# A Mamba-2 scan and a low-rank mixer on one core: U, V and the first weights loaded in another order

## The chip, the core and the metric

The kernel runs on one NeuronCore of a Trainium2 chip. The metric is the device time of one execution in microseconds (us); a kernel's time is the median of its runs. Five engines work beside each other, each through its own instruction stream in order: PE multiplies matrices, DVE and ACT work on elements, POOL does the same more slowly, and SP issues the DMAs. An instruction at the head of an engine's stream that waits holds up everything behind it on that engine.

## The reference

Four sequences (`batch` 4) with 8 heads, 768 positions, head dimension 32 and state size 16 go through a chunked state-space scan; its output is the input of a mixer:

```python
cum = np.cumsum(log_a[chunk]);  L = exp(cum_i - cum_j) * causal
y   = ((C @ B^T) * L) @ x  +  (C @ state) * exp(cum)
state = exp(sum) * state + sum_j B_j x_j * exp(cum_end - cum_j)
# y: (4, 768, 256) after the heads are joined; U (768, 32), V (32, 768)
h = y^T @ U @ V
u = y + h^T
out = u + max(u @ w_ch1, 0) @ w_ch2        # w_ch1 (256, 1024), w_ch2 (1024, 256)
```

The weights U, V, w_ch1 and w_ch2 come as float64. The kernel loads them as pairs of 32-bit words and turns them into float32 by integer and float operations on DVE and ACT.

## The kernel before, in words

**Pairs.** The scan takes two blocks of 128 positions at a time. There are 12 such pairs, three for each sequence, numbered k = 0 to 11, so "the third pair" is k = 2 and "the fourth" k = 3. The first three (sequence 0) go through a form of the scan with larger products (`LIGHT`).

**A plan of words.** One string, `PLAN`, lists all steps in the order in which they are issued; `follow` goes through it, and there is no other scheduler. Each word is a letter and indices. The words that the change and the prediction speak of:

- loads on SP's queue: `b3.0`, `b3.1`, `b3.2` (B and C of k = 3, lines 205 and 210), `x3.0`, `x3.1` (x of k = 3, line 219), `W0`, `W1` (the two halves of the first quarter of w_ch1), `Z` (V), `z` (U), `w3` and on (the other quarters, 512 KB each);
- scan: `Q` and `P` scale B and C by the decays (line 490), `V` and `T` transpose them on PE and copy them out by ACT (lines 506, 510, 516), `g` forms the grams C B^T (lines 537 and 547), `m` and `M` mask them on DVE (lines 569 and 579; for k < 3 the last quarter of a mask goes over ACT and POOL, lines 563 to 567), `s` and `u` update the state, `n`, `i`, `j` build y, `y` copies it out, `O` and `t` turn it into token order;
- weights: `c0` to `c9` convert words to float32, one of four steps at each mention (lines 438 to 453). `c0` and `c2` are the two halves of the first quarter of w_ch1, `c1` is U and V together;
- mixer: `p0`, `q0` project y by U, `v` spreads V, `a0.0` adds h to y (DVE, "yT" at line 772), and `U0.0.1` and the like are the first products with w_ch1 (line 797, tiles "w1f").

**DMAs.** All loads are issued by SP, one after the other. Each DMA uses one of eight completion semaphores in turn, and waits for the DMA that used it before, so that the ninth transfer cannot be issued before the first has landed. U and V share a tile of words and are converted together, so that `c1` needs both. Before the change:

```python
def load_v():
    own["UV"] = words_of(UV)
    weights[1] = UV, own["UV"]
    for q in range(4):
        begin(out=own["UV"][ts(q, Q), 2 * NC * RK:], in_=V2[:, ts(q, 2 * NC * RK)])
```

Loads whose word is B, X, w or L wait in addition for the last DVE instruction that stands ahead of them in the plan; the words b, x, W, z and Z do not.

Of the kernel before, what the change touches and what calls it, by code (L numbers as in the profile page):

```python
# [38 lines left out]
SETTLED = range(4, 12)  # L39
PLAN = (  # L40
# [46 lines left out]
def kernel(  # L87
# [28 lines left out]
    P = 128  # L116
    NB, NH, S, D = x.shape
    N = B.shape[-1]
    NC = S // P
    NPR = NC // 2  # L120
    DM = NH * D
    RK = moe_U.shape[1]
# [7 lines left out]
    Q = 32  # L130
# [27 lines left out]
    class Kept:  # L158
# [6 lines left out]
        def __getattr__(self, name):  # L165
# [16 lines left out]
        out=a_sb,  # L182
        in_=a.rearrange("(g b) h (c s) -> g (b h c) s", g=2, s=P).rearrange(
            "g r s -> r g s"))
# [4 lines left out]
    def hold(load, until):  # L189

        tc.add_manual_dep(load.ins, until.ins.name, mybir.DependencyInfo(
            mybir.DependencyClass.Sync, mybir.DependencyReason.DATA))

    def begin(**kwargs):
        op = nc.sync.dma_start(**kwargs)  # L195
        if until:
            hold(op, until.pop())
# [26 lines left out]
    UV = const.tile([P, 2, NC * RK], FP32)  # L224
# [8 lines left out]
    w2 = [const.tile([P, NM, DM], FP32R, name=f"w2{i}") for i in range(2)]  # L233
    weights = {}
# [7 lines left out]
    def words_of(dst):  # L242
        p, i, j = dst.shape
        t = raw.tile([P, 2 * WCOLS], INT32, tag="words", name="words", bufs=NWORDS)
        return t[:p, :2 * i * j]
# [11 lines left out]
    U2, V2, w12, w22 = (w.bitcast(INT32) for w in (moe_U, moe_V, moe_w_ch1, moe_w_ch2))  # L257
# [2 lines left out]
    w13 = w12.rearrange("(c p) m -> p c m", p=P)  # L260
    own = {}

    def load_v():
        own["UV"] = words_of(UV)
        weights[1] = UV, own["UV"]
        for q in range(4):
            begin(out=own["UV"][ts(q, Q), 2 * NC * RK:], in_=V2[:, ts(q, 2 * NC * RK)])

    def load_u():
        begin(out=own["UV"][:, :2 * NC * RK].rearrange("p (c r) -> p c r", c=NC),  # L270
                          in_=U2.rearrange("(c p) r -> p c r", p=P))

    def load_w(n):
        if n < 2:
# [13 lines left out]
    def load(k):  # L288
        if k < NB * NPR:
            load_bc(k)  # L290
            load_x(k)

    loads = dict(B=load_bc, X=load_x, w=load_w, b=lambda k, p: load_bc(k, (p,)),
                 x=lambda k, c: load_x(k, (c,)), W=load_w, Z=lambda n: load_v(),
                 z=lambda n: load_u())
    for word in LOADS.split():
        loads[word[0]](*(int(v) for v in word[1:].split(".")))
# [36 lines left out]
    for half in range(2):  # L334
        both = sides[:, half].rearrange("p (g s r) -> p s g r", g=2, s=2)
        for s in range(2):
            nc.gpsimd.tensor_scalar(
                out=both[:, s], in0=same[:, None, :].to_broadcast([P, 2, Q]),
# [10 lines left out]
    for g in range(2):  # L349
# [3 lines left out]
        out=la.rearrange("p b c h -> p b h c"),  # L353
# [577 lines left out]
    def ytokens_kept(k):  # L931
# [9 lines left out]
                 v=spread)  # L941
# [51 lines left out]
```

## Time and profile before

| | |
|---|---|
| median of 3 runs | 218.69 us (217.45 to 219.2) |
| the profiled execution's own time | 216.94 us |
| its span, first to last instruction | 215.1 us |
| mean granted PE clock | 1.0 |
| busy share of the span: PE, DVE, ACT, POOL | 96%, 75%, 56%, 7% |
| DMA | 14.57 MB, 69519 packets, of which 63792 under 512 B |

The span is a little shorter than the execution's time, by what lies before the first and after the last instruction (1.84 us here). A row of the timeline gives start and duration in us, engine, line, operation, tiles with shapes, the count of merged instructions, and in brackets how long the engine had idled before it and what ended that. A row of a window gives the busy time of each engine in it, the granted clock, the mean busy share of the 16 DMA engines and the rate. "L169" is the helper through which every DVE instruction of the kernel is issued.

### The profile page before, as it was taken

What the parts mean: (1) busy time and instruction counts of PE and PEld (TensorE: products, weight loads), DVE (VectorE), ACT (ScalarE), POOL (GpSimd) and SP (SyncE); (2) the same over time, 40 slices, a digit from 0 to 9 for tenths busy, and PEclk for the clock granted to TensorE, in tenths of its full rate; (3) what the DMA queues carried; (4) which work ended last, traced back from release to release, by engine and by line L of the source; (5) the groups of instructions that cost most, each with busy time, mean ns of one, the idle gap of its engine ahead of it and who ended that gap; (6) DMA issues with size and microseconds to landing.
All of it is one profiled execution on the core that took longest, in us unless ns stands there. A gap on an engine that the chain in (4) does not pass through costs nothing.

```text
span 215.1 us, 6853 instructions
## 1 busy us (share of the span) xinstructions
PE 207.0 (96%) x2912; PEld 180.8 (84%) x2912; DVE 161.3 (75%) x334; ACT 119.9 (56%) x273; POOL 14.5 (7%) x46
## 2 busy tenths in 40 slices
PE   7998699999999999999999999999999999999993
PEld 4666465666676989999899999998999999999993
DVE  4679499999999999968977594497347756636942
ACT  3566567896847695655275527433646357357120
POOL 7463210000000000000000000000000000000000
PEclk9999999999999999999999999999999999999999
DMA  5987899998850035002061010100001000100012
GB/s 87 142 184 106 120 202 316 155 265 110 109 80 3 2 66 111 0 3 76 3 81 21 24 49 3 49 27 6 6 0 49 0 27 0 49 29 0 0 50 100
DMA packets 69519, 14.57 MB, mean 68 GB/s; under 512 B 63792, under 2 KB 67696, under 8 KB 69488
## 3 DMA queue, kind: packets, MB, share of 16 engines
q1 hardware_dynamic: 69488, 14.13, 33.6%
q8 instruction: 23, 0.38, 0.8%
q14 instruction: 8, 0.07, 0.1%
HBM read 10.98 MB, written 3.15 MB: 66 GB/s over the span
## 4 chain that ended last, share of the span: by engine, by line
PE 84%; SPq 5%; DMA 4%; DVE 2%; issue 2%; ACT 1%; DVEq 0%
PE x L797 31%; PE z L797 24%; PE y L797 12%; SPq L195 5%; PE y L704 3%; PE y L672 3%; DMA words<-in_moe_w_ch_dram 3%; PE x L547 2%; PE w L728 2%; PE w L506 2%; DMA bc<-in_C_dram 2%; PE w L598 1%; PE w L751 1%; PE z L547 1%; DVE M L169 1%
## 5 line engine op out<-in xcount | busy, mean ns | idle before, releaser
L169 DVE SCALAR_TENSOR_TENSOR words<-words 128x768 fp32r<-128x768 f32 (+6 forms) x48 | 38.0, 818 | 0.7 <-PE y L797 0.5
L797 PE MATMUL z<-u,w 128*128 128x384 f32 x144 | 32.0, 341 | 0.0
L797 PE MATMUL x<-u,w 128*128 128x384 f32 x144 | 31.7, 338 | 0.0
L797 PEld LDWEIGHTS z<-u,w 128*128 128x128 f32 x144 | 24.3, 188 | 0.3 <-issue 0.2
L797 PEld LDWEIGHTS x<-u,w 128*128 128x128 f32 x144 | 24.3, 188 | 0.2
L802 ACT ACTIVATE x<-x 128x384 f32<-128x384 f32 (+1 forms) x32 | 14.3, 448 | 18.1 <-PE x L797 18.1
L802 ACT ACTIVATE z<-z 128x384 f32<-128x384 f32 (+1 forms) x28 | 12.8, 461 | 16.6 <-PE z L797 16.1
L169 DVE SCALAR_TENSOR_TENSOR words<-x,words 128x384 fp32r<-128x384 f32 x24 | 13.1, 553 | 8.7 <-ACT words L831 8.6
L169 DVE SCALAR_TENSOR_TENSOR words<-z,words 128x384 fp32r<-128x384 f32 x24 | 12.9, 552 | 8.9 <-ACT words L831 8.8
L797 PE MATMUL y<-w,words 128*128 128x256 f32 x144 | 19.3, 281 | 0.0
L797 PEld LDWEIGHTS y<-w,words 128*128 128x128 f32 x144 | 18.4, 189 | 0.1
L797 PE MATMUL x<-w,words 128*128 128x256 f32 x128 | 18.3, 281 | 0.0
L797 PE MATMUL x<-w2c,words 128*128 128x256 f32 x96 | 17.6, 317 | 0.0
L797 PEld LDWEIGHTS x<-w,words 128*128 128x128 f32 x128 | 17.0, 188 | 0.2
L797 PEld LDWEIGHTS x<-w2c,words 128*128 128x128 f32 x96 | 14.9, 189 | 1.1
L831 ACT ACTIVATE words<-x 128x384 fp32r<-128x384 f32 x24 | 11.7, 491 | 6.0 <-PE x L797 5.9
L831 ACT ACTIVATE words<-z 128x384 fp32r<-128x384 f32 x24 | 11.6, 492 | 3.0 <-PE z L797 3.0
L169 DVE SCALAR_TENSOR_TENSOR S<-S,kept,w 128x64 f32<-128x64 f32 x40 | 11.1, 278 | 1.6
L797 PE MATMUL z<-yT,w1f 128*128 128x384 f32 x32 | 11.7, 495 | 0.1
L797 PE MATMUL x<-yT,w1f 128*128 128x384 f32 x32 | 11.1, 489 | 0.0
L672 PEld LDWEIGHTS y<-T,Sm 32*64 32x64 f32 x352 | 8.1, 131 | 2.7 <-issue 2.1
L797 PE MATMUL y<-w2c,words 128*128 128x256 f32 x72 | 10.3, 282 | 0.0
(170 smaller groups left out, 398.4 us busy)
## 6 DMA issues: line engine op xcount, KB each, us to landing
words<-in_moe_w_ch_dram SPq DMA_DIRECT2D x7, 512.0 KB, 6.8
x<-in_x_dram SPq DMA_DIRECT2D x24, 128.0 KB, 3.6
out_dram<-ytok SPq DMA_DIRECT2D x24, 128.0 KB, 1.7
bc<-in_B_dram SPq DMA_DIRECT2D x24, 64.0 KB, 3.0
bc<-in_C_dram SPq DMA_DIRECT2D x12, 128.0 KB, 3.1
words<-in_moe_w_ch_dram SPq DMA_DIRECT2D x2, 256.0 KB, 5.5
words<-in_moe_V_dram SPq DMA_DIRECT2D x4, 48.0 KB, 4.8
words<-in_moe_U_dram SPq DMA_DIRECT2D x1, 192.0 KB, 5.0
```

What stands on the lines that cost most here:

```text
L169: self.last = call(*args, **kwargs)
L195: op = nc.sync.dma_start(**kwargs)
L506: nc.tensor.transpose(out=tp[:, i, v], in_=s["BC"][:, i, c + v].rearrange("p h n -> p (h n)"), identity=ident)
L547: nc.tensor.matmul(out=g[r][cols, c], lhsT=s["T"][rows, 0, c, cols], rhs=s["Cm"][rows, :, :, ts(2 * c + p, Q)].rearrange("r v t i -> r v i ...
L598: nc.tensor.matmul(out=s["A"][p][ts(r, Q), v], lhsT=s["BC"][half, 0, v, 2 * r:2 * r + 2].rearrange("p h n -> p (h n)"), rhs=x_sb[k][half, ...
L672: product = nc.tensor.matmul(out=y[at][ts(r % 2, H), c, ts(p, H)] if light else y[p][ts(r % 2, H), r // 2, c], lhsT=own[ts(r, Q)], rhs=s[" ...
L704: product = nc.tensor.matmul(out=y[p][ts(i, Q), n, c], lhsT=x_sb[k][half, c, h], rhs=s["M"][half, h // 2, c, h % 2], start=fresh(k, p, [i] ...
L728: nc.tensor.transpose(out=t[:, c, g], in_=yT[b][:, g, ts(2 * q + c, P)], identity=ident)
L751: nc.tensor.matmul(out=p[ts(i % 4, Q), h], lhsT=U_sb[:, c], rhs=ytok[b][:, c, h], start=i < 4, stop=True, skip_group_check=True)
L797: nc.tensor.matmul(out=t, lhsT=lhsT, rhs=rhs, start=start, stop=True, skip_group_check=True)
L802: nc.scalar.activation(t, t, AF.Copy, scale=1.0 + EPS)
L831: nc.scalar.activation(gs[j, m // 2][0][:, m % 2], t, AF.Relu, scale=NEAR)
```

## The change

The third pair's x (both blocks) is loaded ahead of the two halves of the first quarter of w_ch1. U follows directly, then V, and only then the fourth pair's B, C and x. V comes in one transfer of 192 KB whose source is walked as 4 x 32 rows of 1.5 KB, not in four of 48 KB. Of the 650 words of the plan the 21st to the 197th stand in another order; the words themselves are the same, and from `u6.0` on, shortly ahead of `U0.1.0`, the plan is unchanged.

```diff
     own = {}
 
+    def words_uv():
+        if "UV" not in own:
+            own["UV"] = words_of(UV)
+            weights[1] = UV, own["UV"]
+        return own["UV"]
+
     def load_v():
-        own["UV"] = words_of(UV)
-        weights[1] = UV, own["UV"]
-        for q in range(4):
-            begin(out=own["UV"][ts(q, Q), 2 * NC * RK:], in_=V2[:, ts(q, 2 * NC * RK)])
+        v = words_uv()[:, 2 * NC * RK:]
+        begin(out=v, in_=V2.rearrange("r (q c) -> q r c", q=4))
 
     def load_u():
-        begin(out=own["UV"][:, :2 * NC * RK].rearrange("p (c r) -> p c r", c=NC),
-                          in_=U2.rearrange("(c p) r -> p c r", p=P))
+        begin(out=words_uv()[:, :2 * NC * RK].rearrange("p (c r) -> p c r", c=NC),
+              in_=U2.rearrange("(c p) r -> p c r", p=P))
...
 PLAN = (
...
-    'u0.1 W1 W0 Z0 Q2.2 F2.3 x2.0 F3.3 V1.0.2 b3.2 x2.1 b3.0 Q2.1 b3.1 F3.0 z0 x3.0 x3.1 Q2.0 '
+    'u0.1 x2.0 x2.1 W1 Q2.2 F2.3 W0 F3.3 V1.0.2 z0 Z0 b3.2 Q2.1 b3.0 F3.0 b3.1 x3.0 V1.1.2 Q2.0 '
```

On SP's queue, from the load of the second pair's last x block (`x1.0`) on, the rows were these ("waits" names the semaphore that the row waits for, DMAHW0 to DMAHW7 being those of the DMAs):

```order
L195 DMA x<-in_x_dram 128x8x32 [waits DMAHW5_49]
L195 DMA words<-in_moe_w_ch_dram 128x2x256 [waits DMAHW6_49]
L195 DMA words<-in_moe_w_ch_dram 128x2x256 [waits DMAHW7_49]
L195 DMA words<-in_moe_V_dram 32x384 [waits DMAHW0_49]
L195 DMA words<-in_moe_V_dram 32x384 [waits DMAHW1_49]
L195 DMA words<-in_moe_V_dram 32x384 [waits DMAHW2_49]
L195 DMA words<-in_moe_V_dram 32x384 [waits DMAHW3_49]
L195 DMA x<-in_x_dram 128x8x32 [waits DMAHW4_49]
L195 DMA bc<-in_B_dram 128x8x16 [waits DMAHW5_49]
L195 DMA x<-in_x_dram 128x8x32 [waits DMAHW6_49]
L195 DMA bc<-in_B_dram 128x8x16 [waits DMAHW7_49]
L195 DMA bc<-in_C_dram 128x8x32 [waits DMAHW0_49]
```

Behind the last of them came U and the fourth pair's x, twice. Now the same place reads:

```order
L195 DMA x<-in_x_dram 128x8x32 [waits DMAHW5_49]
L195 DMA x<-in_x_dram 128x8x32 [waits DMAHW6_49]
L195 DMA x<-in_x_dram 128x8x32 [waits DMAHW7_49]
L195 DMA words<-in_moe_w_ch_dram 128x2x256 [waits DMAHW0_49]
L195 DMA words<-in_moe_w_ch_dram 128x2x256 [waits DMAHW1_49]
L195 DMA words<-in_moe_U_dram 128x6x64 [waits DMAHW2_49]
L195 DMA words<-in_moe_V_dram 128x1x384 [waits DMAHW3_49]
L195 DMA bc<-in_B_dram 128x8x16 [waits DMAHW4_49]
L195 DMA bc<-in_B_dram 128x8x16 [waits DMAHW5_49]
L195 DMA bc<-in_C_dram 128x8x32 [waits DMAHW6_49]
L195 DMA x<-in_x_dram 128x8x32 [waits DMAHW7_49]
L195 DMA x<-in_x_dram 128x8x32 [waits DMAHW0_49]
```

U has moved ahead of the fourth pair's B and C, V takes one place of the eight and not four, and the weights have two x blocks in front of them.

On DVE, between the first mask and the conversion of U and V, stood before (masks are the rows with "lower", state updates those of S; 128x256 are `c0` and `c2`, 128x384 is `c1`):

```order
L169 TENSOR_TENSOR words<-z,lower 128x512
L169 TENSOR_TENSOR words<-x,lower 128x512 x2
L169 TENSOR_SCALAR words<-words 128x256 x2
L169 SCALAR_TENSOR_TENSOR S<-S,kept,w 128x64 x2
L169 TENSOR_SCALAR words<-words 128x256 x2
L169 SCALAR_TENSOR_TENSOR S<-S,kept,w 128x64 x2
L169 TENSOR_TENSOR words<-z,lower 128x512
L169 TENSOR_TENSOR words<-x,lower 128x512 x2
L169 SCALAR_TENSOR_TENSOR S<-S,kept,w 128x64 x3
L169 SCALAR_TENSOR_TENSOR words<-words 128x256 x2
L169 TENSOR_SCALAR words<-words 128x384 x2
L169 SCALAR_TENSOR_TENSOR w1f<-words 128x2x128
```

(the first two rows twice, for two pairs). Now:

```order
L169 TENSOR_TENSOR words<-x,lower 128x512 x4
L169 TENSOR_TENSOR words<-z,lower 128x512 x2
L169 SCALAR_TENSOR_TENSOR S<-S,kept,w 128x64 x4
L169 TENSOR_SCALAR words<-words 128x256 x2
L169 TENSOR_TENSOR words<-z,lower 128x512
L169 TENSOR_TENSOR words<-x,lower 128x512 x2
L169 SCALAR_TENSOR_TENSOR S<-S,kept,w 128x64 x2
L169 TENSOR_SCALAR words<-words 128x256 x2
L169 SCALAR_TENSOR_TENSOR S<-S,kept,w 128x64
L169 TENSOR_SCALAR words<-words 128x384 x2
L169 SCALAR_TENSOR_TENSOR words<-words 128x256 x2
L169 SCALAR_TENSOR_TENSOR w1f<-words 128x2x128
```

The first conversion step (`c0`, now the half `W0`) stands behind six masks and four state updates, the second half behind three more masks. From the first mask to the first "yT" addition DVE has the same instructions in both orders.

20 rows, old and new, of the table PLAN are left out of this document.

## The prediction

> **What bounds the kernel now.** I read the busy shares first, then the stages by windows, then what each engine waits for in the one stage that is not full.
>
> ```profile
> PE 207.0 (96%) x2912; PEld 180.8 (84%) x2912; DVE 161.3 (75%) x334; ACT 119.9 (56%) x273; POOL 14.5 (7%) x46
> 12.03:21.81 9.78, 9.02 (x287) 6.33 (x275) 9.15 (x22) 6.59 (x18) 4.32 (x9) 1.00 0.76 151
> 21.81:24.41 2.60, 1.70 (x40) 1.35 (x40) 0.00 (x1) 0.20 (x2) 1.10 (x1) 1.00 0.69 107
> 24.41:32.02 7.61, 6.29 (x176) 4.17 (x176) 7.07 (x20) 5.71 (x16) 0.72 (x2) 1.00 0.97 174
> 12.03:32.02 19.99, 17.00 (x497) 11.86 (x482) 16.22 (x42) 12.50 (x34) 6.14 (x12) 1.00 0.83 154
> 32.64:60.00 27.36, 27.36 (x460) 17.88 (x461) 26.61 (x64) 22.55 (x49) 0.25 (x2) 1.00 0.95 189
> 60.00:200.00 140.00, 140.00 (x1754) 132.53 (x1752) 103.55 (x192) 77.15 (x172) 0.59 (x6) 1.00 0.13 28
> ```
>
> The columns of a window are its length, then busy time of PE, PE's weight loads, DVE, ACT and POOL, the granted clock, the DMA share and GB/s. From 32.64 to 200 us PE is busy without a gap at a clock of 1.00, so whatever lets that stage begin earlier ends the kernel earlier by as much, as long as nothing later runs dry. Before it there is room: in the 19.99 us from DVE's first mask to its first yT addition DVE works 16.22 and idles 3.77, and 2.60 of that is one piece, in which ACT works for only 0.20.
>
> ```profile
> 19.18 0.58 SPq L195 DMA_DIRECT2D words<-in_moe_U_dram  x1
> 24.30 0.55 ACT L442 ACTIVATE words<-words 128x384 f32<-128x384 uint32 x1 [2.40 <-issue]
> 24.41 0.63 DVE L169 TENSOR_SCALAR words<-words 128x384 int32<-128x384 int32 x2 [2.60 <-DMA x<-in_x_dram]
> 25.84 0.60 ACT L510 COPY T<-w 128x512 f32<-128x512 f32 x1
> 27.23 0.35 PE L547 MATMUL x<-Cm,T 32*64 32x128 f32 x2 [0.68 <-ACT Cm L516]
> 28.12 0.76 DVE L169 TENSOR_TENSOR M<-z,causal 128x256 int32<-128x256 int32 x2 [0.30 <-PE z L547]
> 32.02 0.56 DVE L169 TENSOR_TENSOR yT<-x,yT 128x384 f32<-128x384 f32 x1
> 32.64 1.56 PE L797 MATMUL z<-yT,w1f 128*128 128x384 f32 x4
> words<-in_moe_U_dram SPq DMA_DIRECT2D x1, 192.0 KB, 5.0
> ```
>
> Both engines wait at `c1`, the conversion of U and V (128x384). The profile names the x transfer, but that is of other data. U was issued at 19.18 and takes 5.0, so it lands at about 24.2, and ACT and DVE go on at 24.30 and 24.41. Behind `c1` in ACT's stream stands the copy of the fourth pair's transpose (25.84); its gram on PE waits for that (27.23), and the gram's masks on DVE (28.12) are on the way to yT (32.02), after which the first mixer product starts (32.64).
>
> **Why U is late.**
>
> ```profile
> 9.82 0.66 SPq L195 DMA_DIRECT2D x<-in_x_dram  x1
> 10.52 1.09 SPq L195 DMA_DIRECT2D words<-in_moe_w_ch_dram  x2
> 11.66 2.69 SPq L195 DMA_DIRECT2D words<-in_moe_V_dram  x4
> 16.05 0.98 SPq L195 DMA_DIRECT2D x<-in_x_dram  x1
> 18.55 0.58 SPq L195 DMA_DIRECT2D bc<-in_C_dram  x1
> 19.81 1.74 SPq L195 DMA_DIRECT2D x<-in_x_dram  x2
> 21.66 2.28 SPq L195 DMA_DIRECT2D bc<-in_B_dram  x1
> 10.52 5.51 DMA words<-in_moe_w_ch_dram
> 16.05 0.45 ACT L442 ACTIVATE words<-words 128x256 f32<-128x256 uint32 x1 [0.79 <-DMA words<-in_moe_w_ch_dram]
> 16.75 0.44 ACT L442 ACTIVATE words<-words 128x256 f32<-128x256 uint32 x1 [0.25 <-DMA words<-in_moe_w_ch_dram]
> ```
>
> Four V issues cost SP 2.69 us and four of the eight places. The x block at 16.05 stands eight places behind the first weight half, and leaves when that has landed (10.52 + 5.51 = 16.03). U is issued only after it and three more transfers.
>
> **The change part by part.** *U and V earlier.* In the new queue eight places before U lies the third pair's C, long landed, so U needs no landing to be issued: two x blocks and two weight halves after 10.52 at about 0.55 to 0.66 each put it at 13 us, 6 earlier. With the 5.0 it takes now it lands at 18, with another 2 for traffic at 20; V follows it. DVE comes to `c1` at about 21.0 (worked out below, under the weights). The 2.60 wait goes: **-2.60**.
>
> *One transfer for four.* SP saves three issues, 3 x 0.67 = 2.0 us; U's 0.58 now stands ahead of the fourth pair's C. So C is issued near 18.55 - 2.0 + 0.6 = 17.1 and lands 3.54 later, at 20.7 and not at 22.1.
>
> ```profile
> 18.55 3.54 DMA bc<-in_C_dram
> 22.22 1.10 POOL L490 TENSOR_TENSOR BC<-bc,F 128x512 f32<-128x512 f32 x1 [0.70 <-DMA bc<-in_C_dram]
> 25.26 0.35 PE L598 MATMUL w<-x,BC 64*32 64x64 f32 x16 [0.16 <-DMA x<-in_x_dram]
> 5.00:10.00 5.00, 4.57 (x60) 3.38 (x59) 3.31 (x11) 2.43 (x8) 2.32 (x8) 1.00 1.08 150
> 12.00:16.00 4.00, 4.00 (x134) 2.77 (x126) 3.68 (x6) 2.76 (x8) 2.22 (x5) 1.00 0.74 198
> 34.00:36.00 2.00, 2.00 (x8) 1.17 (x7) 1.90 (x4) 1.66 (x4) 0.00 (x0) 1.00 1.04 392
> ```
>
> POOL's scaling (22.22) and the fourth pair's state products, which wait for x (25.26), move up by 1 to 2 us with it. With ACT no longer held at `c1` the gram is there when DVE comes to its masks, so the 0.30 at 28.12 goes too: **-0.30**. If it does not, 0.
>
> *Weights behind the third pair's x.* This is the price. Two x blocks, 262 KB, now pass ahead of `W1` and `W0`. At the 150 GB/s of the stretch in which the DMA engines were full (5 to 10 us, share 1.08) that is 1.75 us; but from 12 to 16 us the engines were only 0.74 busy, and about 1.0 us of it falls into that gap. I take 0.75, between 0 (all in the gap) and 1.75. `W0` lands now just ahead of 16.75 and would land at 17.5. DVE comes to it after six masks and four state updates:
>
> ```profile
> 12.64 1.28 DVE L169 TENSOR_TENSOR words<-x,lower 128x512 int32<-128x512 int32 x2
> 13.83 0.68 DVE L169 TENSOR_TENSOR words<-z,lower 128x512 int32<-128x512 int32 x1
> 16.05 0.50 DVE L169 TENSOR_SCALAR words<-words 128x256 int32<-128x256 int32 x2 [0.34 <-DMA words<-in_moe_w_ch_dram]
> 16.46 0.66 DVE L169 SCALAR_TENSOR_TENSOR S<-S,kept,w 128x64 f32<-128x64 f32 x2
> 19.90 0.92 DVE L169 SCALAR_TENSOR_TENSOR S<-S,kept,w 128x64 f32<-128x64 f32 x3
> 20.74 1.07 DVE L169 SCALAR_TENSOR_TENSOR words<-words 128x256 f32<-128x256 f32 x2
> ```
>
> Masks follow each other at 0.60 (two from 12.64 to 13.83) and updates at 0.28 (three from 19.90 to 20.74): 12.03 + 3.6 + 1.1 = 16.75. So the wait for the weights, 0.34 now, becomes 0.75, **+0.41**; by the bounds it is 0 to 1.75, that is -0.34 to +1.41. Behind this wait stand, on DVE, the third pair's masks, for which its products on PE wait; ACT's first conversion step waits with it. From there three masks, three updates and two conversion steps at 0.41 (16.05 to 16.46) follow until `c1`: 17.5 + 0.41 + 1.8 + 0.85 + 0.41 = 21.0.
>
> *The order of the other words.* It moves no work between engines. Conversions, masks and state updates before yT are the same set, 16.22 us, so yT cannot start before 12.03 + 16.22 = 28.25, a gain of at most 3.77. Behind yT the two orders carry the same DVE work up to the last quarter of w_ch1, and the later weights (`w3` and on) are free to be issued sooner. I take 0, bounds -0.3 to +0.8: PE is full there, and DVE with 26.61 of 27.36 nearly so, so that a bad swap would show at once.
>
> **The sum** is -2.60 - 0.30 + 0.41 = -2.5: yT at 29.5, the first mixer product at 30.1, a span of 212.6, and 214.4 in place of the profiled execution's 216.94. That execution is 1.75 under the median of the runs shown, so the median goes from 218.69 to **216.2**. By the bounds of the weights, the masks and the order it lies between 215.2 (-2.60 - 0.30 - 0.34 - 0.3) and 218.3 (-2.60 + 1.41 + 0.8).
>
> **Rivals.** *V on four of the DMA engines.* The one transfer walks its source as 4 x 32 rows; if the work is dealt out by that outer 4, four engines carry all of it. At the 392 GB/s that all 16 moved from 34 to 36 us, four would move 98: 196.6 KB take 2.0 us and not 0.5, and what is queued behind on these engines, the fourth pair's parts, comes 1.5 later. V itself would land at 20 to 21, about when DVE wants it, at 21.0. C would be at 22, x at 24.5, the gram about 0.8 behind the masks' turn: a gain of 1.7, and with some luck less, **217.2**. For it speaks the shape; against it that the destination has 128 rows. The Trainium skill, "DMA: Bandwidth & Descriptors", section "Rules for kernel authors", speaks against the change here: it says that the slowest dimension of both sides sets how many engines a transfer uses, so that an outer dimension under 16 confines it. If that rule holds here, 217.2 is the time; no row of the trace before shows a transfer of this shape.
>
> *The gain is given back.* DVE is 97% busy from 32.64 to 60, and PE's first products need a converted quarter of w_ch1 each. Were a quarter late after the swap of conversions, PE would idle there by what it came earlier: **218.7**. Against it: DVE itself comes to these conversions 2.5 earlier, and the quarters can be issued earlier.
>
> *Slower: the fourth pair starves behind U and V.* In the old queue SP was stuck for 2.28 us at the issue at 21.66 and 1.74 for the two before, right behind U, so a lagging engine can hold the whole queue. With U and V one after the other this could hit C and x of the fourth pair. Its gram must reach DVE by 28.12, as now, for the time to stay; that is so up to an x that lands at about 27, 2 us later than now. Stuck twice as long as now, x would come at 29.3, and the kernel at **221.0**. Against it: SP has 2.0 us less to issue there and three more places.
>
> **How the numbers follow.** The forecast has 0.55, V on four engines 0.20, given back 0.15, slower 0.10. One per cent, 2.19 us, is about what a measurement of this kernel can tell from no change; below 216.5 is faster, above 220.9 slower. The forecast's centre lies 0.3 below the first bound and gives faster at 0.65 of its chance, the four-engine case at 0.3, which makes 0.36 + 0.06 and with a little from the third case 0.44. The slower case gives 0.08, and 0.03 comes from the others: 0.11. The rest, 0.45, is the same. The range reaches from 214.3, the lower bound with the 0.9 by which the runs before differ, to 219.3, which takes in the second and third case and leaves the slower one out.
>
> **What would show it.** In the profile after: SP issues U at about 13 us; the 2.60 of DVE and 2.40 of ACT at `c1` are gone; DVE waits 0 to 1.75 for the first weights at about 17; the first "yT" addition starts near 29.5 and the first product of line 797 (there 801) near 30.1; from there PE has no gap. I am wrong if PE's first mixer product starts earlier by 2 us or more and the span does not shrink by it, or if DVE's idle time before yT has only moved, to the weights or to the fourth pair's gram.

## The result and the profile after

The changed kernel takes **220.73 us** (median of 6 runs, 219.99 to 221.77), the kernel before in the same session 218.37 us (217.34 to 219.2). The ratio is **1.0138, 95% interval [1.0106, 1.0171]**: slower, by 2.4 us in the medians and by 3.0 in the ratio and between the profiled executions (219.99 and 216.94). I had forecast 2.5 us less; the time lies outside my range.

From the page of the changed kernel, its busy shares and its granted clock in 40 slices, then the windows that answer to those of before (first mask to yT, first mixer product to the product that needs `w4`, and on to the end):

```profile
span 218.3 us, 6849 instructions
PE 209.1 (96%) x2912; PEld 182.0 (83%) x2912; DVE 162.6 (74%) x334; ACT 120.0 (55%) x273; POOL 14.4 (7%) x46
PEclk9999999999999999999999999999999999999999
12.70:32.79 20.09, 17.07 (x495) 11.76 (x480) 17.30 (x43) 13.02 (x36) 6.16 (x12) 1.00 0.81 144
33.54:49.57 16.03, 14.48 (x206) 8.77 (x204) 14.06 (x30) 11.59 (x26) 0.00 (x0) 1.00 1.00 251
60.00:200.00 140.00, 139.73 (x1845) 131.56 (x1844) 104.35 (x196) 77.57 (x172) 0.69 (x7) 1.00 0.14 30
```

From 60 to 200 us PE is as full as before. The loss lies ahead of that. The stretch from the first mask to yT takes 20.09 us, where before took 19.99: nothing was gained. DVE idles 2.79 of it and no longer 3.77, but the same instructions keep it busy for 17.30 instead of 16.22. The next stretch takes 16.03, and here PE works only 14.48. Before, the same products stood in this window, in which PE never paused:

```profile
32.64:46.60 13.96, 13.96 (x205) 8.86 (x205) 13.75 (x30) 12.07 (x28) 0.00 (x0) 1.00 0.97 244
```

So the product at the end of the window comes at 49.57 instead of 46.60, 3.0 us later, and the span is 3.2 longer (218.3 against 215.1). Of the 3.0, 0.9 are there at the first product (33.54 against 32.64), and 1.55 are PE's pauses behind it. DVE's and PE's rows in the timeline of the changed kernel show where:

```profile
12.70 2.48 DVE L169 TENSOR_TENSOR words<-x,lower 128x512 int32<-128x512 int32 x4 [1.76 <-POOL BC L494]
19.00 0.50 DVE L169 TENSOR_SCALAR words<-words 128x256 int32<-128x256 int32 x2 [1.42 <-DMA words<-in_moe_w_ch_dram]
22.54 0.94 DVE L169 TENSOR_SCALAR words<-words 128x384 int32<-128x384 int32 x2
24.53 1.32 DVE L169 SCALAR_TENSOR_TENSOR words<-words 128x256 f32<-128x256 f32 x1
29.09 0.76 DVE L169 TENSOR_TENSOR M<-x,causal 128x256 int32<-128x256 int32 x2 [0.21 <-PE z L551]
31.60 0.43 DVE L169 TENSOR_TENSOR ps<-w,ps 64x256 fp32r<-64x256 f32 x1 [0.49 <-ACT ps L765]
32.79 0.56 DVE L169 TENSOR_TENSOR yT<-x,yT 128x384 f32<-128x384 f32 x1
39.77 0.77 DVE L169 TENSOR_SCALAR words<-words 128x512 int32<-128x512 int32 x2 [1.83 <-DMA words<-in_moe_w_ch_dram]
25.62 0.66 PE L510 MATMUL w<-ident,BC 128*128 128x128 f32 x4 [1.18 <-POOL BC L494]
33.54 2.75 PE L801 MATMUL z<-yT,w1f 128*128 128x384 f32 x8
40.92 1.56 PE L801 MATMUL z<-yT,w1f 128*128 128x384 f32 x4 [0.47 <-DVE M L169]
45.93 1.53 PE L801 MATMUL x<-yT,w1f 128*128 128x384 f32 x4 [0.87 <-DVE w1f L169]
49.57 1.56 PE L801 MATMUL z<-yT,w1f 128*128 128x384 f32 x4
```

The wait at `c1` (22.54, 128x384), which was 2.60, is gone as forecast. In its place stand 1.42 at the first weights (19.00) and 0.49 at "ps" (31.60), and `c1` itself comes 1.5 later than I had it (21.0), though 1.87 earlier than before (24.41). That is lost again behind it: from `c1` to yT took 7.61 before and takes 10.25 now. One conversion step lasts 1.32 there (24.53), where its like take 0.42; why, these rows do not tell. PE waits 1.18 for the fourth pair's scaled B and C (25.62; 0.90 before), since its C landed at 24.29 and not at 22.10. Then comes a wait that I had given nothing: 1.83 us for `w4` (39.77), the quarter of w_ch1 that DVE converts third. The masks and the conversion that stand behind it on DVE end PE's waits of 0.47 at 40.92 and 0.87 at 45.93. Of the first mask's 0.67 I make nothing: in the profiled executions of all the kernels below it stands between 11.8 and 12.8, in either order.

The chain of waits of the changed kernel names two transfers, V and `w4`; SP's rows show the queue around V:

```profile
16.21 6.24 DMA words<-in_moe_V_dram
33.14 6.60 DMA words<-in_moe_w_ch_dram
12.81 2.84 SPq L195 DMA_DIRECT2D words<-in_moe_w_ch_dram  x2
15.70 0.47 SPq L195 DMA_DIRECT2D words<-in_moe_U_dram  x1
16.21 0.71 SPq L195 DMA_DIRECT2D words<-in_moe_V_dram  x1
18.72 3.43 SPq L195 DMA_DIRECT2D bc<-in_C_dram  x1
```

U is issued at 15.70, not at 13, because SP sat 2.33 us at the first weights (12.81). V lands at 22.45 (16.21 + 6.24), just ahead of `c1`. The fourth pair's C is held up for 3.43 us in SP's queue. In both of these long issues the transfer that had used the same semaphore had landed long before (at 9.79 and at 15.81): no landing that the issue had to wait for explains them.

### The profile page after: what moved, and what is told of

The parts are those of the page before. It is cut to its first block, busy times and chain, and to the rows that moved or that the text cites. A ratio compares the mean times of both kernels' runs of the same rounds, so it can differ in the third digit from the quotient of the medians.

```text
span 218.3 us, 6849 instructions
## 1 busy us (share of the span) xinstructions
PE 209.1 (96%) x2912; PEld 182.0 (83%) x2912; DVE 162.6 (74%) x334; ACT 120.0 (55%) x273; POOL 14.4 (7%) x46
## 4 chain that ended last, share of the span: by engine, by line
PE 79%; SPq 7%; DMA 6%; DVE 5%; ACT 2%; issue 1%; ACTq 0%; DVEq 0%
PE x L801 28%; PE z L801 21%; PE y L801 12%; SPq L195 6%; PE y L708 3%; DMA words<-in_moe_w_ch_dram 3%; DVE words L169 3%; DMA words<-in_moe_V_dram 3%; PE y L676 3%; PE w L732 2%; PE x L551 2%; PE w L602 1%; PE w L510 1%; PE w L755 1%; DVE M L169 1%; PE w L763 1%
## 5 line engine op out<-in xcount | busy, mean ns | idle before, releaser
L169 DVE SCALAR_TENSOR_TENSOR words<-words 128x768 fp32r<-128x768 f32 (+6 forms) x48 | 38.7, 831 | 1.0 <-PE y L801 0.5
L806 ACT ACTIVATE z<-z 128x384 f32<-128x384 f32 (+1 forms) x28 | 12.8, 461 | 16.2 <-PE z L801 15.7
L169 DVE SCALAR_TENSOR_TENSOR words<-z,words 128x384 fp32r<-128x384 f32 x24 | 12.9, 552 | 9.1 <-ACT words L835 9.0
L169 DVE SCALAR_TENSOR_TENSOR words<-x,words 128x384 fp32r<-128x384 f32 x24 | 13.1, 554 | 8.8 <-ACT words L835 8.7
L169 DVE SCALAR_TENSOR_TENSOR S<-S,kept,w 128x64 f32<-128x64 f32 x40 | 11.1, 278 | 1.6
L801 PE MATMUL z<-yT,w1f 128*128 128x384 f32 x32 | 11.8, 496 | 0.5 <-DVE M L169 0.5
L676 PE MATMUL y<-T,Sm 32*64 32x64 f32 x352 | 10.5, 234 | 0.8 <-issue 0.8
```

What stands on the lines that cost most here:

```text
L169: self.last = call(*args, **kwargs)
L676: product = nc.tensor.matmul(out=y[at][ts(r % 2, H), c, ts(p, H)] if light else y[p][ts(r % 2, H), r // 2, c], lhsT=own[ts(r, Q)], rhs=s[" ...
L801: nc.tensor.matmul(out=t, lhsT=lhsT, rhs=rhs, start=start, stop=True, skip_group_check=True)
L806: nc.scalar.activation(t, t, AF.Copy, scale=1.0 + EPS)
```

## The experiments

Theory A: V on few DMA engines holds up the queue behind it. Theory B: `w4`, loaded behind `w2` and `w5`, is late. Rival C: the third pair's x ahead of the weights makes them late. Each ratio is to the kernel before, run on the same chip in the same session. In the later diffs only the load words are shown, in their order on SP's queue; the computing words stay in the order that the text names. They stop at `w7`; where they show all late loads, the four loads behind it change places too (`X6 L9 L7 L8` in the old order, `L8 X6 L9 L7` in the new). `w2`, `w3` and `w4` are the other three quarters of w_ch1, `w5` to `w8` are parts of w_ch2, all of 512 KB. `x4.0` and `x4.1` are the x of the fifth pair (k = 4, in the second sequence); some expectations call it the fourth sequence's x. A plan with a line more or less shifts the line numbers by one (L168 for L169).

**V in four transfers, in the changed kernel** (`after_v4`).

```diff
-        begin(out=v, in_=V2.rearrange("r (q c) -> q r c", q=4))
+        for q in range(4):
+            begin(out=v[ts(q, Q)], in_=V2[:, ts(q, 2 * NC * RK)])
```

> The changed kernel with V again in four transfers of 32 rows, in the same place of the queue. Theory A (the one transfer runs on four DMA engines, takes some 3.5 us of their time and holds SP's queue): V lands within 4 us of its issue, SP's issue of the fourth pair's C is under 1.5 us and not 3.4, the first yT addition moves from 32.8 to 30.5 to 31.5, and the time falls by 1.0 to 2.5 us from the changed kernel's 220.7. Rival C (the two x blocks ahead of the weights are the cause, since DVE waits 1.4 us for W0): three more issues on SP make it no better, yT stays within 0.5 us of 32.8 and the time within 0.7 us of 220.7.

1.0105 [1.0069, 1.014]. The interval overlaps that of the changed kernel. In the profile, of an execution of 221.61 us where the median is 218.88, the issue of the fourth pair's C still sits 2.59 us, where under 1.5 was expected, and yT comes at 32.51, not at 30.5 to 31.5.

**V in one transfer, in the kernel before** (`before_v1`).

```diff
-        for q in range(4):
-            begin(out=own["UV"][ts(q, Q), 2 * NC * RK:], in_=V2[:, ts(q, 2 * NC * RK)])
+        begin(out=own["UV"][:, 2 * NC * RK:], in_=V2.rearrange("r (q c) -> q r c", q=4))
```

> The kernel before with the one edit that V comes in one transfer, all words in their old order. Theory A: V takes over 5 us from issue to landing, the issues behind it are held for 2 us and more, and the time rises by 0.5 to 2.5 us over 218.4, although three issues are saved. If the transfer is not confined, the three issues and three places saved bring U forward by about 2 us and the time falls by 1 to 2 us.

0.9978 [0.9946, 1.001]. V by itself shows no cost here. It is slower (see the last section), and SP sits 4.16 us at the third pair's second x block (13.82), the third issue behind V, as theory A expected; but SP issues three transfers less, and in the profile U lands at 22.96 instead of 24.23 and yT comes at 31.23 instead of 32.02. Theory A does not explain the loss.

**`w2` and `w4` exchanged, in the changed kernel** (`after_w4`).

```diff
-w3 b5.1 b5.2 w2 w5 w4 w6 x4.1 B6 X5 w8 x4.0 w7
+w3 b5.1 b5.2 w4 w5 w2 w6 x4.1 B6 X5 w8 x4.0 w7
```

> The changed kernel with the loads w2 and w4 exchanged in the plan, so that the quarter of w_ch1 that DVE converts second (w4) is second in the queue again and not fourth. Theory B (DVE's 1.83 us wait at 39.77 for w4 holds the masks behind it and PE runs dry): that wait goes, and the time falls by 1.3 to 2.2 us from 220.7. If PE would have been late anyway (theory A alone), the time stays within 0.6 us.

1.0119 [1.0068, 1.017]: the wait for `w4` is gone from the profile and hardly anything is gained. **Both edits together** (`after_v4_w4`), V in four and `w4` first:

> Both: V in four transfers and w2 and w4 exchanged. Theories A and B together: the two gains add to 3 to 4.5 us, 216.2 to 217.7, at or below the kernel before. If both edits cure the same lateness, the gain is that of the larger one alone, 218.5 to 219.5.

1.0163 [1.0113, 1.0214], no gain at all. Theories A and B had both failed as they stood. Theory D then: the order of the loads as a whole, against E, the order of the computing words. Five kernels separate the two, and the loads ahead of the fourth pair's x from those behind it. All have V in one transfer.

**The old computing order with all loads in the new order** (`before_newloads`).

```diff
-W1 W0 Z0 x2.0 b3.2 x2.1 b3.0 b3.1 z0 x3.0 x3.1
-b4.0 b4.1 b4.2 b5.1 b5.0 w3 b5.2 w4 w5 w2 x4.1 w6 x4.0 X5 B6 w8 w7
+x2.0 x2.1 W1 W0 z0 Z0 b3.2 b3.0 b3.1 x3.0 x3.1
+b4.1 b5.0 b4.2 b4.0 w3 b5.1 b5.2 w2 w5 w4 w6 x4.1 B6 X5 w8 x4.0 w7
```

> The old order of all computing words, with the load words in the new order (V in one transfer): what the new order of the loads does by itself, to be read against the old order with V in one transfer, which stood at 0.998 of the kernel before. Theory D (the order of the loads makes the loss, in two places: the fourth pair's C and x land 1 to 2 us later behind U, V and the third pair's x, and w4 and the fourth sequence's x land behind w2, w5 and w8): 1.010 to 1.018 of the kernel before, 2 to 4 us slower, with the third stage product of x (z<-yT, third quarter) as late as in the changed kernel, 3 us. Rival E (the order of the masks, conversions and updates makes it): 0.997 to 1.002.

1.0106 [1.0046, 1.0165], as theory D has it and clear of E; the product that stands at 45.81 in `before_v1` comes at 49.25, 3.4 us later.

**The new computing order with all loads in the old order** (`after_oldloads`).

```diff
-x2.0 x2.1 W1 W0 z0 Z0 b3.2 b3.0 b3.1 x3.0 x3.1
-b4.1 b5.0 b4.2 b4.0 w3 b5.1 b5.2 w2 w5 w4 w6 x4.1 B6 X5 w8 x4.0 w7
+W1 W0 Z0 x2.0 b3.2 x2.1 b3.0 b3.1 z0 x3.0 x3.1
+b4.0 b4.1 b4.2 b5.1 b5.0 w3 b5.2 w4 w5 w2 x4.1 w6 x4.0 X5 B6 w8 w7
```

> The new order of the computing words with the load words in the old order (V in one transfer). Theory D: within 0.4% of the kernel before (0.996 to 1.004), U's wait at DVE stays near 2 us, w4 lands at about 37 to 38 us. Rival E: 1.010 to 1.016, since the late conversions stand in the new order. My prediction's own step for the order (0, bounds -0.3 to +0.8 us) says 0.995 to 1.002.

1.0039 [1.0001, 1.0077], in D's range, with E's 1.010 outside the interval.

**The old order, only the front loads new** (`before_front`).

```diff
-W1 W0 Z0 x2.0 b3.2 x2.1 b3.0 b3.1 z0 x3.0 x3.1
+x2.0 x2.1 W1 W0 z0 Z0 b3.2 b3.0 b3.1 x3.0 x3.1
```

> The old order of the computing words; of the loads only those up to the fourth pair's second x in the new order (third pair's x, then weights, U, V, then the fourth pair's B, C, x), later loads as before. Theory D: the DMA engines set this stage, the fourth pair's C lands at 23.5 to 24.5 us and x at 26.5, yT 0.5 to 1.5 us later than with V in one transfer alone: 1.002 to 1.006 of the kernel before. My prediction's step (U's wait goes, C lands earlier): yT 2 us earlier, 0.989 to 0.992. If the place makes nothing: 0.997.

1.0046 [1.0003, 1.0089], the fourth pair's C landed at 23.35 us.

**The old order, only the late loads new** (`before_late`).

```diff
-b4.0 b4.1 b4.2 b5.1 b5.0 w3 b5.2 w4 w5 w2 x4.1 w6 x4.0 X5 B6 w8 w7
+b4.1 b5.0 b4.2 b4.0 w3 b5.1 b5.2 w2 w5 w4 w6 x4.1 B6 X5 w8 x4.0 w7
```

> The old order of the computing words and of the loads up to the fourth pair's x (V in one transfer); only the loads behind it in the new order, where w4 stands behind w2 and w5, and the fourth sequence's first x behind B6, X5 and w8. Theory D, if the parts add: the front loads made 0.7% (1.0046 against 0.998), all the loads 1.3% (1.0106), so these make 0.6%: 1.002 to 1.006, yT as with V in one transfer alone, a wait of 0.5 to 1.5 us at the fourth sequence's x, the third quarter's product of x 1 to 2 us later than there. Rival: the late loads are harmless as long as the first stage is not late: 0.996 to 1.000.

1.0140 [1.0098, 1.0182], well over the 1.002 to 1.006 expected: the parts do not add. The late loads by themselves cost the old order as much as the whole change costs. In the profile, of an execution of 221.67 us where the median is 220.23, DVE waits 4.47 us for `w4`, PE 2.33 behind that, and PE 0.84 for `x4.0`.

**The changed kernel, only the late loads old** (`after_oldlate`).

```diff
-b4.1 b5.0 b4.2 b4.0 w3 b5.1 b5.2 w2 w5 w4 w6 x4.1 B6 X5 w8 x4.0 w7
+b4.0 b4.1 b4.2 b5.1 b5.0 w3 b5.2 w4 w5 w2 x4.1 w6 x4.0 X5 B6 w8 w7
```

> The changed kernel with the late loads in the old order and its front loads kept: against the new computing order with all loads old (1.004) it shows what the front loads cost in the new order. If as much as in the old order (0.7%): 1.009 to 1.012. If the new computing order fits them (it was written for them): 1.002 to 1.006, as with w4 and the fourth sequence's x put back (1.0047).

1.0031 [0.9996, 1.0067]: the front loads show no cost in the new order. Together:

| front loads | late loads | old computing order | new computing order |
|---|---|---|---|
| old | old | 0.9978 [0.9946, 1.0010] | 1.0039 [1.0001, 1.0077] |
| new | old | 1.0046 [1.0003, 1.0089] | 1.0031 [0.9996, 1.0067] |
| old | new | 1.0140 [1.0098, 1.0182] | not run |
| new | new | 1.0106 [1.0046, 1.0165] | 1.0138 [1.0106, 1.0171] |

In the right column the step from old to new late loads is 1.1%, with intervals that lie apart. In the left one it is 1.6% with the old front loads and 0.6%, with intervals that overlap, with the new ones. The computing order by itself makes 0.6% (0.9978 to 1.0039), with intervals that overlap a little.

**Which late load it is.** Three kernels in the old order with the late loads new, in which one or both of the displaced transfers are put back.

```diff
-w2 w5 w4 w6 x4.1 B6 X5 w8 x4.0 w7
+w4 w5 w2 w6 x4.1 B6 X5 w8 x4.0 w7
```

> The old order with the new order of the late loads, and only w4 put back ahead of w2 and w5. If w4 is the cause: its wait of 4.47 us at DVE goes, the fourth sequence's x stays late, 1.003 to 1.007 of the kernel before. If x is the one that gates: its wait grows from 0.84 to 2 or 3 us, and the time stays at 1.010 to 1.014.

1.0159 [1.0106, 1.0213]: `w4` alone gives nothing back. PE's rows in the timeline and the DMA's piece in the chain show what took its place; the third row is the same step in `before_v1`, without a wait:

```profile
44.63 4.67 DMA x<-in_x_dram
49.35 1.11 PE L601 MATMUL w<-x,BC 64*32 64x64 f32 x56 [3.77 <-DMA x<-in_x_dram]
44.35 0.79 PE L597 MATMUL w<-x,BC 64*32 64x64 f32 x56
```

The state products of the fifth pair wait 3.77 us for `x4.0`. It is issued at 44.63, behind `B6`, `X5` and `w8`. SP sits 2.14 us at the first load of `B6`, until a DVE instruction that it has to wait for is done (35.99), and 5.28 us at the second. That one's semaphore had been free since 32.67; five 512-KB weights had been issued ahead of it, and its issue ends (41.64) shortly before the last of them lands (41.83). That it was held up behind them is what this suggests; it is not shown. SP's rows:

```profile
28.18 5.26 SPq L194 DMA_DIRECT2D words<-in_moe_w_ch_dram  x4
33.50 0.57 SPq L194 DMA_DIRECT2D x<-in_x_dram  x1
34.17 2.14 SPq L194 DMA_DIRECT2D bc<-in_B_dram  x1
36.36 5.28 SPq L194 DMA_DIRECT2D bc<-in_C_dram  x1
41.68 0.58 SPq L194 DMA_DIRECT2D bc<-in_B_dram  x1
42.31 1.26 SPq L194 DMA_DIRECT2D x<-in_x_dram  x2
43.67 0.91 SPq L194 DMA_DIRECT2D words<-in_moe_w_ch_dram  x1
44.63 0.47 SPq L194 DMA_DIRECT2D x<-in_x_dram  x1
```

In `before_v1` it lands at 40.75, 3.6 us before PE wants it. Now the other one put back:

```diff
-w2 w5 w4 w6 x4.1 B6 X5 w8 x4.0 w7
+w2 w5 w4 w6 x4.0 x4.1 B6 X5 w8 w7
```

> The same with only the fourth sequence's first x put back, ahead of its second and of B6, X5 and w8; w4 stays behind w2 and w5. If w4 is the cause: 1.009 to 1.014, a wait of 3 to 4.5 us at its conversion. If x is the cause: 1.002 to 1.005.

1.0070 [1.0036, 1.0104]. PE's rows show no wait for `x4.0`, and DVE waits 1.00 for `w4`, which PE does not feel:

```profile
37.95 0.76 DVE L168 TENSOR_SCALAR words<-words 128x512 int32<-128x512 int32 x2 [1.00 <-DMA words<-in_moe_w_ch_dram]
33.17 0.55 PE L509 MATMUL w<-ident,BC 128*128 128x128 f32 x3 [1.33 <-issue]
38.98 2.75 PE L800 MATMUL z<-yT,w1f 128*128 128x384 f32 x8
45.96 0.79 PE L601 MATMUL w<-x,BC 64*32 64x64 f32 x56
47.34 1.56 PE L800 MATMUL z<-yT,w1f 128*128 128x384 f32 x4
```

It falls between my two expectations, 1.009 to 1.014 (`w4` the cause) and 1.002 to 1.005 (x the cause), and its interval reaches into both. For x speaks that the intervals of the two kernels, with `w4` and with x put back, lie apart, and that `w4` alone gained nothing. What is left is in this profile mostly the 1.33 "issue", which is no wait for a load of the plan (last section): the last product shown comes at 47.34, in `before_v1` at 45.81. How late `w4` is depends on more than its place: it landed at 37.93 here and at 41.83 in `before_late`, with the same queue ahead of it.

Both put back:

```diff
-w2 w5 w4 w6 x4.1 B6 X5 w8 x4.0 w7
+w4 w5 w2 w6 x4.0 x4.1 B6 X5 w8 w7
```

> Both put back, the rest of the late loads in the new order. If these two places are all that the late order does: as V in one transfer alone, 0.995 to 1.001, with no wait over 0.5 us between 33 and 50 us. If the rest counts too: 1.003 to 1.008.

1.0062 [1.0024, 1.0101], as with x alone. So of the two, x is the one that counts in the old order. What keeps this kernel above 0.998 is only partly known: its profile has no wait for a late load before 50 us, but 0.41 "issue", and PE had waited 1.88 for the third pair's x at 21.51. Single profiles also scatter: in the four kernels of the old order with new late loads all that stands ahead of the first yT is the same but for the order of two weights of equal size, and yT came at 31.61, 31.97, 32.03 and 32.95.

**The same two put back in the changed kernel** (`after_w4_x4`).

```diff
-w2 w5 w4 w6 x4.1 B6 X5 w8 x4.0 w7
+w4 w5 w2 w6 x4.0 x4.1 B6 X5 w8 w7
```

> The changed kernel with only its two late loads put back to earlier places: w4 ahead of w2, and the fourth sequence's first x ahead of the second. Theory D: both late waits (1.83 us at w4's conversion, 2.3 us at x behind it) are gone, 2 to 3 us faster than the changed kernel, 1.000 to 1.004 of the kernel before, with what the first stage loses (yT 0.8 us later) left over. If the late loads were only followed by another wait: 1.010 to 1.014, as with w4 alone.

1.0047 [1.0009, 1.0085], against 1.0119 with `w4` alone and 1.0138 with neither; 1.000 to 1.004 was expected. The two together bring most of the loss back. That putting back `w4` only uncovered x is my reading and not shown: PE waits 2.33 for x at 48.87 in the profile of `after_v4_w4`, but not in that of `after_w4`, and x alone was not put back in the changed kernel.

**The front order, part by part**, in the old order with V in one transfer and all late loads old.

```diff
-W1 W0 Z0 x2.0 b3.2 x2.1 b3.0 b3.1 z0 x3.0 x3.1
+W1 W0 Z0 x2.0 b3.2 x2.1 z0 b3.0 b3.1 x3.0 x3.1
```

> What the change seemed to be for, by itself: the old order with V in one transfer, and only U moved, two places forward, ahead of the fourth pair's B and C. My prediction's step: DVE and ACT come to c1 without a wait, C as early as before, 0.990 to 0.994. Theory D (the bytes on the DMA engines set the stage; U forward puts C and x back by its own 1 us): U lands 1 us earlier, C 0.5 to 1 us later, 0.997 to 1.002.

0.9990 [0.9969, 1.0011]: U two places earlier, as the change wants it, gains nothing. Against `before_v1` U landed at 21.36 and not at 22.96, the fourth pair's C at 22.38 and not at 22.08, and the first yT came at 31.12 and not at 31.23. These are PE's rows of it: the third pair's x is waited for, then the grams go on as in `before_v1`.

```profile
20.34 0.32 PE L601 MATMUL w<-x,BC 64*32 64x64 f32 x8 [1.14 <-DMA x<-in_x_dram]
23.70 0.66 PE L509 MATMUL w<-ident,BC 128*128 128x128 f32 x4 [0.30 <-POOL BC L493]
```

So the third pair's x alone was moved ahead of V:

```diff
-W1 W0 Z0 x2.0 b3.2 x2.1 b3.0 b3.1 z0 x3.0 x3.1
+W1 W0 x2.0 x2.1 Z0 b3.2 b3.0 b3.1 z0 x3.0 x3.1
```

> The old order with V in one transfer, and the third pair's x moved ahead of V but not ahead of the weights; U and the fourth pair's parts at their places. Theory D: x lands at 18 us and not at 20.4, PE's wait for it (1.27 us with V in one transfer) and DVE's behind it go; V lands later without harm, U at 23 as before: 0.993 to 0.998, the earliest yT of these kernels. Rival (whatever is moved forward, what stands behind it comes as much later and gates too): 0.997 to 1.003.

1.0026 [0.9996, 1.0056]. x landed at 17.56 and PE's wait for it went, but other waits came in its place: U landed at 23.55, DVE waited 2.50 for it, PE 2.38 for the fourth pair's C.

```profile
23.67 0.99 DVE L168 TENSOR_SCALAR words<-words 128x384 int32<-128x384 int32 x2 [2.50 <-DMA words<-in_moe_U_dram]
24.23 0.65 PE L509 MATMUL w<-ident,BC 128*128 128x128 f32 x4 [2.38 <-POOL BC L493]
34.31 0.55 PE L509 MATMUL w<-ident,BC 128*128 128x128 f32 x3 [2.45 <-issue]
```

And with the weights ahead of x, otherwise as the front loads of the change:

```diff
-x2.0 x2.1 W1 W0 z0 Z0 b3.2 b3.0 b3.1 x3.0 x3.1
+W1 W0 x2.0 x2.1 z0 Z0 b3.2 b3.0 b3.1 x3.0 x3.1
```

> As before_front, but with the weights ahead of the third pair's x: weights, x, U, V, then the fourth pair's B, C, x. It tells the two parts of the front order apart. If it is U and V ahead of the fourth pair (theory D): as before_front, 1.002 to 1.006, C of the fourth pair at 23 to 24 us. If it is x ahead of the weights: as V in one transfer alone, 0.996 to 1.000.

1.0053 [1.0022, 1.0083], as with x ahead of them (1.0046): rival C falls in the old order, and in the new one the front loads as a whole show no cost. C lands at 23.47 here, and 23.35 there, against 22.08 in `before_v1`. That U and V ahead of the fourth pair make the old order's 0.7% is not shown: x alone ahead of V stands at 1.0026, between the two, with intervals that overlap, and the half clock of the last section may have a share in 1.0046. No kernel of the study is faster than before by more than the interval; V in one transfer comes nearest.

## Why the prediction was wrong, step by step

- **What bounds the kernel**: right as far as it went. PE from the first mixer product on sets the end, and what comes late there stays: 3.0 us at the product of 49.57, 3.2 in the span.
- **U and V earlier, -2.60**: the wait at `c1` went, and yT did not come earlier (32.79 against 32.02). This step failed: it counted the wait as a price that nothing else stands behind. U, which was to leave at 13 since no landing held it, left at 15.70; `c1` began 1.87 earlier than before, and the way from there to yT was 2.64 longer. Of DVE's idle time 1.42 now stood at the weights (0.34 before), which I had named as a sign of being wrong. In the kernel with U moved alone, yT came 0.1 us earlier; where x was moved alone, the wait went to U and C. My reading is that in this stage the third pair's x, the weights, U and the fourth pair's C and x are each wanted almost as soon as they land, so that an order only chooses which wait shows.
- **One transfer for four; C lands at 20.7**: failed. It landed at 24.29 (22.10 before): its issue began at 18.72 and sat 3.43 us, until shortly before V had landed. The step counted issues, at 0.67 each, and not that an issue can sit. With only this edit C landed at 22.08, as before, and the 0.998 can't be told from no change.
- **Weights behind the third pair's x, wait 0.75 by my value, 1.75 by its bound**: right in kind, 1.42 measured, which is +1.08 and not +0.41 in the sum. `W0` landed at 18.98, where I had 17.5.
- **The mask's wait, -0.30**: 0.21 remained.
- **The same DVE work before yT, 16.22**: the same instructions, but 17.30 of busy time; 0.90 of it is the step at 24.53.
- **The order of the other words, 0, bounds -0.3 to +0.8**: this is the step that failed most. I looked at the computing words and wrote that the later weights "are free to be issued sooner". The same edit put two 512-KB weights (`w2`, `w5`) ahead of `w4`, and one (`w8`) with `B6` and `X5` ahead of `x4.0`. With the late loads in their old order the changed kernel stands at 1.0031, with them new at 1.0138: 1.1% of 218 is 2.3 us. With x and `w4` alone put back it is 1.0047, 2.0 us.
- **The computing order**: 0.6%, 1.3 us, of which I had nothing, though not clear of the noise; why is open. In profiles of kernels with it, old loads or new, a wait of 0.49 for "ps" stands in DVE's rows (here with all loads old), and U's and the gram's waits before it:

```profile
23.28 0.67 DVE L168 TENSOR_SCALAR words<-words 128x384 int32<-128x384 int32 x2 [1.62 <-DMA words<-in_moe_U_dram]
29.36 0.76 DVE L168 TENSOR_TENSOR M<-x,causal 128x256 int32<-128x256 int32 x2 [0.92 <-PE z L550]
31.86 0.43 DVE L168 TENSOR_TENSOR ps<-w,ps 64x256 fp32r<-64x256 f32 x1 [0.49 <-ACT ps L764]
```

- **The rivals**: "V on four engines" was right about the transfer, as far as its packets tell, and wrong about its price. "The gain is given back" named the place, a quarter of w_ch1 late, but took it as a limit on the gain and let it cost nothing of its own. "The fourth pair starves behind U and V", 221.0, came nearest in number; its mechanism, C held up behind U and V, is seen, but the front loads that bring it stand only 0.7% above the old ones in the old order and show no cost in the new. The bulk is another one, so that the number came near by luck.

The four steps from the kernel before to the changed one are V in one transfer -0.2%, the computing order +0.6%, the front loads -0.1%, the late loads +1.1%; this is one way through the table, and the left column shows that another gives other shares. Only the last of the four is clear of the noise.

## What to carry to other kernels

Where one queue feeds everything, an order of steps is also an order of transfers: list, for every transfer that moves back, when it will now land and what wants it first, also far behind the place that the change is about. A wait for a transfer in a stage that is full of transfers is no price to be cashed: look which of the others is wanted within that time. And if one late transfer is put right and nothing is gained, look for the next one on the same queue before giving up the idea.

## What the hardware showed that I had not expected

**A wait of PE, it seems for its own code.** In nine of the profiles PE stops near 32 us with "issue" as the reason, eight times within the same four transposes (line 509, between the first and the other three). In the packet records a 16,384-byte packet of the instruction queue begins ahead of that: at 32.05 in `before_x2`, 31.77 in `before_front`, 30.87 in `before_late_x4`; PE goes on at 34.31, 34.01 and 33.17, and in all nine 2.2 to 2.4 us after the packet's start. In the nine other profiles, those of before and after among them, that packet begins at 27.5 to 29.5, and there is no such wait. The rows are the instruction queue in the 1.4 us from 31.8 in `before_x2`, and the window of the 2 us in which PE did nothing:

```profile
q8 instruction: 1, 0.02, 4.2%
32.00:34.00 2.00, 0.00 (x0) 0.00 (x0) 2.00 (x6) 0.87 (x3) 0.00 (x0) 1.00 0.99 297
```

The DMA share is 0.99. That the code comes through the same full engines and stood in line behind weights is what this suggests; no record tells which engine carried it, and no run took the load away to test it. At 0.4 to 2.45 us it is as large as the effects under study, and it stands in the profile of every kernel of the old order with front or late loads moved, but for `before_u`: part of what the table puts down to loads may come by this way. In the changed kernel and in `after_oldlate` it is absent, so that the 1.1% between these two owe it nothing in the profiles.

**One transfer, few engines.** V's 128 packets of 1,536 B, in four transfers, were up to 14 at once in flight; in one transfer with an outer 4, in the changed kernel, never more than 5 and most often 4, over 3.5 us (18.37 to 21.84). This fits the rule of the Trainium skill, "DMA: Bandwidth & Descriptors", section "Rules for kernel authors", that the slowest dimension sets the number of engines, though no record names the engine of a packet. My 2.0 us for it were too few; and no cost of it is seen in the time (0.998).

**A half clock after a wait.** In the profile of the kernel with `w4` alone put back the granted clock is 0.50 for 3.4 us, beginning 3.3 us after the long wait for x set in:

```profile
48.90:52.30 3.40, 2.95 (x122) 2.48 (x123) 2.01 (x6) 0.12 (x1) 0.00 (x0) 0.50 0.93 154
```

`after_v4_w4` has one of 6.8 us, which began 1.5 us after a pause of 2.33 set in. Six other profiles have one such stretch of 3.4 us, beginning at 19 to 26 us, each 1.1 to 2.7 us after a pause of PE of 0.5 to 2.8 us set in; but pauses of 2.4 us in `before_x2` and `before_x2uv` were followed by none, so what decides is open. The Trainium skill, "TensorE: Matmul & The Clock Gate", Part 1, has the clock at full or half only, in windows of about 3.4 us; the trace agrees with both. So a wait of PE may cost more than its length: the product behind that wait came 5.5 us later than in `before_v1` (51.32 against 45.81), of which 1.3 were there at the first product (33.10 against 31.84), 3.77 is the wait, and about 0.5 is left, which I put down to the slow clock.

The half clock is also spread unevenly over the executions. In `before_front` nine of twelve have a mean granted clock of 0.985 to 0.992, in the kernel before beside it eight of 29. The other three take 216.7 us in the mean, and so do the other 21 of the kernel before; with so few it stays open how much of the 1.0046 is the order of the loads. The loss of the changed kernel is not of this kind: its two executions at a clock of 1.00 take 219.99 and 220.77 us.
